# A one-token attention and MLP block on one core: K loads moved between the query-weight loads, wo and w2 loaded in pieces, w2 in longer rows

## The chip, the cores and the metric

The kernel runs on one core of one Trainium2 chip. The metric is the device time of one execution in microseconds (us); lower is better. All runs told here are fast (within 1.5% of the fastest run of the same kernel), and every one of them was compared with runs of the kernel before made in the same rounds on the same chip. A "span" is the time from the first to the last instruction in a profile; it is about 2 us shorter than the measured time of the same run (83.9 against 85.78 before).

## The reference

One new token goes through a pre-norm attention block with a cached window of 4096 keys and values, then through a pre-norm ReLU MLP. Batch and sequence length are 1, the model width D is 512, there are 32 query heads on 8 key/value heads of size 128, and the MLP is 1792 wide. Everything is bf16.

```python
h  = x + attn(layernorm(x))        # q = xn @ wq; softmax(q k^T / sqrt(128)) v; @ wo
h2 = h + relu(layernorm(h) @ w1) @ w2
```

No tensor is used more than once, so the kernel must read all of it: 4.2 MB of wq, 8 x 1.05 MB each of K and V, 4.2 MB of wo, and 1.8 MB each of w1 and w2, together 28.8 MB.

## The kernel before

All loads go out on one queue (SP) in this order, and there are enough buffers (eight shared by wq and K, eight for V) that they are issued well before they are needed (the median K load 19.9 us before it lands):

```python
nc.sync.dma_start(xr_bf[0:1, :], ...)                    # x, 1 KB
for c in range(DC):                                      # wq in four pieces of 1 MB
    nc.sync.dma_start(wq_sb[c], wq_v[:, c, :])
WO_POS = max(Hkv - 2, 0)                                 # 6
for g in range(Hkv):
    if g == WO_POS:
        nc.sync.dma_start(wo_sb[:, :, :], A_wo.rearrange("(c p) n -> p c n", p=P))   # 4 MB, rows of 1 KB
    load_kv(g)                                           # K_g, then V_g, rows of 8 KB
nc.sync.dma_start(w1_sb[:, :, :], B_w1.rearrange("(c p) n -> p c n", p=P))           # rows of 3.5 KB
nc.sync.dma_start(w2_sb[:, :, :], B_w2.rearrange("(c p) n -> p c n", p=P))           # rows of 1 KB
```

(`wq_sb` stands in short for a list of tiles.) The compute, in the order in which it is written; a scheduler at build time decides the order on each engine by when it expects operands to be ready, and the engine then keeps to that order:

```python
... layernorm of x; q: 128 matmuls of wq (weights) by one column, 32 per piece of wq
for g in range(Hkv):
    group_transposes(g)            # T: 32 transposes of K_g on PE, 4 copies on DVE
    if g >= 1: group_pv(g - 1)     # PV: 32 matmuls with V, then the scaling by the inverse sums
    group_scores(g)                # S: 32 matmuls, exp on ACT, sums, inverse, broadcast
    if g == WO_POS:                # hTg: wo matmuls of groups 0 to 5 together (96)
        while wo_done < g: group_wo(wo_done); wo_done += 1
    elif g > WO_POS and wo_done < g:
        group_wo(wo_done); wo_done += 1
group_pv(Hkv - 1)
while wo_done < Hkv: group_wo(wo_done); wo_done += 1
... layernorm of h
... u: 56 matmuls of w1; relu; y: 56 matmuls of w2 into y_ps, reduced; out = y * rstd + h
... transpose to a row; one PSUM tile, first half copied by DVE, second by ACT; store
```

The softmax here doesn't subtract the row's maximum and nothing guards it: scores larger than these inputs give would overflow.

Of the kernel before, what the change touches and what calls it, by code (L numbers as in the profile page):

```python
# [8 lines left out]
BF16 = mybir.dt.bfloat16  # L9
F32 = mybir.dt.float32  # L10
# [6 lines left out]
def kernel(  # L17
# [12 lines left out]
    nc = tc.nc  # L30
    P = nc.NUM_PARTITIONS

    D = A_x.shape[-1]
    Hq, Dh = 32, 128
    _, Hkv, Sk, Dh2 = A_k_cache.shape
# [3 lines left out]
    rep = Hq // Hkv  # L39
    Dff = B_w1.shape[1]  # L40
    DC = D // P
# [3 lines left out]
    NC = W // P  # L45
# [3 lines left out]
    HC = Hq  # L49
    FC = Dff // P  # L50
# [5 lines left out]
    work = ctx.enter_context(tc.tile_pool(name="work", bufs=1))  # L56
    egp = ctx.enter_context(tc.tile_pool(name="egp", bufs=2))
    ktp = ctx.enter_context(tc.tile_pool(name="ktp", bufs=7))
    kx = ctx.enter_context(tc.tile_pool(name="kx", bufs=8))
    vp = ctx.enter_context(tc.tile_pool(name="vp", bufs=8))  # L60
    wp = ctx.enter_context(tc.tile_pool(name="wp", bufs=1))
    psA = ctx.enter_context(tc.tile_pool(name="psA", bufs=1, space=bass.MemoryType.PSUM))
    psT = ctx.enter_context(tc.tile_pool(name="psT", bufs=3, space=bass.MemoryType.PSUM))
    psS = ctx.enter_context(tc.tile_pool(name="psS", bufs=1, space=bass.MemoryType.PSUM))
    psO = ctx.enter_context(tc.tile_pool(name="psO", bufs=3, space=bass.MemoryType.PSUM))
# [2 lines left out]
    nc.sync.dma_start(xr_bf[0:1, :], A_x.flatten_outer_dims()[0:1, :])  # L68

    wq_v = A_wq.rearrange("(c p) n -> p c n", p=P)  # L70
    wq_sb = []
    for c in range(DC):
        t = kx.tile([P, Hq * Dh], BF16, tag="kx")
        nc.sync.dma_start(t[:, :], wq_v[:, c, :])
        wq_sb.append(t)

    wo_sb = wp.tile([P, HC, D], BF16)
    w1_sb = wp.tile([P, DC, Dff], BF16)
    w2_sb = wp.tile([P, FC, D], BF16)

    Ks = [None] * Hkv
    Vs = [None] * Hkv

    def load_kv(g):
        kt = kx.tile([P, NCC, TK * Dh], BF16, tag="kx")
        nc.sync.dma_start(
            kt[:, :, :],
            A_k_cache[0, g, W0:Sk, :].rearrange("(c p t) d -> p c (t d)", p=P, t=TK),
        )
        Ks[g] = kt  # L90
        vt = vp.tile([P, NCC, TK * Dh], BF16, tag="vt")
        nc.sync.dma_start(
            vt[:, :, :],
            A_v_cache[0, g, W0:Sk, :].rearrange("(c p t) d -> p c (t d)", p=P, t=TK),
        )
        Vs[g] = vt

    WO_POS = max(Hkv - 2, 0)
    for g in range(Hkv):
        if g == WO_POS:  # L100
            nc.sync.dma_start(wo_sb[:, :, :], A_wo.rearrange("(c p) n -> p c n", p=P))
        load_kv(g)
    nc.sync.dma_start(w1_sb[:, :, :], B_w1.rearrange("(c p) n -> p c n", p=P))
    nc.sync.dma_start(w2_sb[:, :, :], B_w2.rearrange("(c p) n -> p c n", p=P))

    ident_bf = consts.tile([P, P], BF16)
    make_identity(nc, ident_bf[:])
# [38 lines left out]
    for c in range(DC):  # L146
        nc.tensor.matmul(
            xT_ps[:, c : c + 1], lhsT=xr_bf[0:1, c * P : (c + 1) * P],
            rhs=ones_col_bf[0:1, 0:1], start=True, stop=True,
# [11 lines left out]
    for c in range(DC):  # L161
        for h in range(Hq):
            nc.tensor.matmul(  # L163
                qT_ps[:, c, h : h + 1],
                lhsT=wq_sb[c][:, h * Dh : (h + 1) * Dh],
                rhs=xnT_bf[:, c : c + 1],
                start=True, stop=True,
# [5 lines left out]
    qTs_bf = work.tile([P, Hq], BF16)  # L173
    nc.vector.tensor_scalar(out=qTs_bf[:, :], in0=qT_f[:, :], scalar1=att_scale, scalar2=None, op0=ALU.mult)

    epart = work.tile([P, Hq], F32)
    rtot = work.tile([1, Hq], F32)
    rtot_bf = work.tile([1, Hq], BF16)
# [2 lines left out]
    hT_acc = work.tile([P, DC], F32)  # L181

    E_tiles = [None] * Hkv
    copy_idx = [0]

    kT_blocks_all = [None] * Hkv

    def group_transposes(g):
        kT_blocks = []
        for b in range(NTB):  # L190
            tp = psT.tile([P, TB, P], BF16)
            for i in range(TB):
                ct = b * TB + i
                c, t = divmod(ct, TK)
                nc.tensor.transpose(  # L195
                    tp[:, i, :], Ks[g][:, c, t * Dh : (t + 1) * Dh], ident_bf[:, :],
                )
            ktb = ktp.tile([P, TB, P], BF16)
            nc.vector.tensor_copy(ktb[:, :, :], tp[:, :, :])  # L199
            kT_blocks.append(ktb)  # L200
        kT_blocks_all[g] = kT_blocks

    def group_scores(g):
        kT_blocks = kT_blocks_all[g]
        ST = psS.tile([P, NC, rep], F32)
        for ct in range(NC):
            b, i = divmod(ct, TB)
            nc.tensor.matmul(  # L208
                ST[:, ct, :],
                lhsT=kT_blocks[b][:, i, :],  # L210
                rhs=qTs_bf[:, rep * g : rep * (g + 1)],
                start=True, stop=True,
            )
        E = egp.tile([P, NC, rep], BF16)
        nc.scalar.activation(out=E[:, :, :], in_=ST[:, :, :], func=ACT.Exp)  # L215
        E_tiles[g] = E
        nc.vector.tensor_reduce(  # L217
            out=epart[:, rep * g : rep * (g + 1)],
            in_=E[:, :, :].rearrange("p c j -> p j c"),
            axis=AX.X, op=ALU.add,  # L220
        )
        tot_ps = psA.tile([1, rep], F32, tag="misc")
        nc.tensor.matmul(  # L223
            tot_ps[0:1, :], lhsT=ones_colf[:, 0:1], rhs=epart[:, rep * g : rep * (g + 1)],
            start=True, stop=True,
        )
        nc.vector.reciprocal(rtot[0:1, rep * g : rep * (g + 1)], tot_ps[0:1, :])  # L227
        nc.vector.tensor_copy(rtot_bf[0:1, rep * g : rep * (g + 1)], rtot[0:1, rep * g : rep * (g + 1)])
        bc_ps = psA.tile([P, rep], F32, tag="misc")
        nc.tensor.matmul(  # L230
            bc_ps[:, :], lhsT=ones_row_bf[0:1, :], rhs=rtot_bf[0:1, rep * g : rep * (g + 1)],
            start=True, stop=True,
        )
        nc.vector.tensor_copy(bc_sb[:, rep * g : rep * (g + 1)], bc_ps[:, :])  # L234

    def group_pv(g):
        E = E_tiles[g]
        OT = psO.tile([P, rep], F32, tag="po")
        for ct in range(NC):
            c, t = divmod(ct, TK)  # L240
            nc.tensor.matmul(  # L241
                OT[:, :], lhsT=Vs[g][:, c, t * Dh : (t + 1) * Dh], rhs=E[:, ct, :],
                start=(ct == 0), stop=(ct == NC - 1),
            )
        nc.vector.tensor_tensor(  # L245
            out=OTn_bf[:, rep * g : rep * (g + 1)], in0=OT[:, :],
            in1=bc_sb[:, rep * g : rep * (g + 1)], op=ALU.mult,
        )
    n_hT = [0]

    def group_wo(g):
        hTg = psO.tile([P, DC], F32, tag="po")
        for m in range(DC):
            for j in range(rep):
                h = rep * g + j
                nc.tensor.matmul(  # L256
                    hTg[:, m : m + 1],
                    lhsT=wo_sb[:, h, m * P : (m + 1) * P],
                    rhs=OTn_bf[:, h : h + 1],
                    start=(j == 0), stop=(j == rep - 1),  # L260
                )
        if n_hT[0] == 0:
            nc.vector.tensor_copy(hT_acc[:, :], hTg[:, :])
        else:
            nc.vector.tensor_tensor(out=hT_acc[:, :], in0=hT_acc[:, :], in1=hTg[:, :], op=ALU.add)  # L265
        n_hT[0] += 1

    wo_done = 0
    for g in range(Hkv):
        group_transposes(g)  # L270
        if g >= 1:
            group_pv(g - 1)
        group_scores(g)
        if g == WO_POS:
            while wo_done < g:
                group_wo(wo_done)
                wo_done += 1
        elif g > WO_POS and wo_done < g:
            group_wo(wo_done)
            wo_done += 1  # L280
    group_pv(Hkv - 1)
    while wo_done < Hkv:
        group_wo(wo_done)
        wo_done += 1

    hT_f = work.tile([P, DC], F32)
    nc.vector.tensor_tensor(out=hT_f[:, :], in0=hT_acc[:, :], in1=xT_f[:, :], op=ALU.add)
# [7 lines left out]
    uT_ps = psA.tile([P, DC, FC], F32, tag="misc")  # L295
    for c in range(DC):
        for m in range(FC):
            nc.tensor.matmul(  # L298
                uT_ps[:, c, m : m + 1], lhsT=w1_sb[:, c, m * P : (m + 1) * P],
                rhs=hc_bf[:, c : c + 1], start=True, stop=True,  # L300
            )
    uT_f = work.tile([P, FC], F32)
# [6 lines left out]
    for c in range(FC):  # L309
        for m in range(DC):  # L310
            nc.tensor.matmul(  # L311
                y_ps[:, c, m : m + 1], lhsT=w2_sb[:, c, m * P : (m + 1) * P],
                rhs=uT_bf[:, c : c + 1], start=True, stop=True,
# [5 lines left out]
    outT_bf = work.tile([P, DC], BF16)  # L319
# [1 line left out]
        out=outT_bf[:, :], in0=yT_f[:, :], scalar=rstd2[:, 0:1], in1=hT_f[:, :],  # L321
        op0=ALU.mult, op1=ALU.add,
    )
    orow_ps = psA.tile([1, D], F32, tag="misc")
    for c in range(DC):
        nc.tensor.matmul(  # L326
            orow_ps[0:1, c * P : (c + 1) * P], lhsT=outT_bf[:, c : c + 1], rhs=ident_bf[:, :],
            start=True, stop=True,
        )
    orow_bf = work.tile([1, D], BF16)  # L330
    hD = D // 2
    nc.vector.tensor_copy(orow_bf[0:1, 0:hD], orow_ps[0:1, 0:hD])  # L332
    nc.scalar.copy(orow_bf[0:1, hD:D], orow_ps[0:1, hD:D])  # L333
    nc.sync.dma_start(out.flatten_outer_dims()[0:1, :], orow_bf[0:1, :])


# [28 lines left out]
```

## Time and profile before

| | before |
|---|---|
| time, median of all 15 runs beside the changed kernel | 85.69 us (85.04 to 86.07) |
| span | 83.9 us |
| last byte of K/V, w1, w2 moved | 66.1, 70.6, 75.7 us |
| last landing (completion of w2) | 76.2 us |
| u starts, y ends | 75.9, 79.8 us |

First the slices of the profile page: the span of 83.9 us is cut into 40 slices of 2.1 us, each digit is the busy share in tenths, and the last row is what the DMA engines moved in GB/s.

```profile
PE   0113444079799799799799799869997799637730
DMA  0999999999999999999999999999999999970000
GB/s 0 289 422 422 430 434 422 422 422 418 418 430 418 414 418 426 410 422 414 430 364 348 348 349 354 364 408 422 418 414 413 395 400 363 348 224 6 8 0 0
```

The load stream never rests from 2.1 to about 75 us. It moves at about 420 GB/s, except for one valley of 348 from slice 20 to slice 25 (counted from 0), which is wo with its rows of 1 KB, and a decline at the end, which is w1 and w2. After the stream there are 8 us in which nothing is loaded. PE is lightly used up to slice 7 and nearly full from slice 8 on.

Next the timeline of PE in the kernel before. Columns: start, duration (us), engine, line and operation, output<-inputs, shapes, count, and in brackets how long PE sat idle before it and what ended that.

```profile
13.46 1.01 PE L163 MATMUL qT_ps<-xnT_bf,t 128*128 128x1 bf16 x32 [1.47 <-DMA t<-in_A_wq_dram]
17.38 3.60 PE L195 MATMUL tp<-ident_bf,kt 128*128 128x128 bf16 x32 [2.91 <-DMA kt<-in_A_k_cache_dram]
...
23.89 3.60 PE L195 MATMUL tp<-ident_bf,kt 128*128 128x128 bf16 x32
...
30.40 3.59 PE L195 MATMUL tp<-ident_bf,kt 128*128 128x128 bf16 x32
...
56.71 2.72 PE L256 MATMUL hTg<-OTn_bf,wo_sb 128*128 128x1 bf16 x96 [0.59 <-DMA wo_sb<-in_A_wo_dram]
59.30 3.57 PE L195 MATMUL tp<-ident_bf,kt 128*128 128x128 bf16 x32
...
75.92 1.63 PE L298 MATMUL uT_ps<-hc_bf,w_sb 128*128 128x1 bf16 x56 [0.95 <-DVE hc_bf L291]
78.16 1.63 PE L311 MATMUL y_ps<-uT_bf,w_sb 128*128 128x1 bf16 x56 [0.61 <-DVE uT_bf L307]
```

The transposes of group 0 wait for K0, which stands behind all of wq. From there a group follows every 6.51 us (6.20 once, before group 5), without a wait for data. The one exception: before the transposes of group 6 stand 96 wo matmuls, and they waited 0.59 us for wo. After hT (the last wo matmul ends at 74.1) come the layernorm, u and y, one after the other, all of it behind the end of the stream.

### The profile page before, as it was taken

To read this page: it belongs to the slowest core of one execution; us is meant where nothing else is said; L and a number is where in the kernel's file an instruction comes from. 1 tells how busy PE (TensorE), PEld (TensorE's weight loads), DVE (VectorE), ACT (ScalarE), POOL (GpSimd) and SP (SyncE) were. 2 spreads that over 40 slices of the span, in tenths; PEclk is the share of its full clock that TensorE was granted. 3 is DMA by queue.
4 is the path that set the end of the run, shared out by engine and by line. 5 is a ranking of instruction groups with operands and counts; after the bars stand their busy time and mean duration, and the time that the engine had idled before them with its cause. 6 is when DMAs were issued, how large, how long until landed. Compare 5 with 4: busy or idle time off the path is not lost.

```text
span 83.9 us, 2563 instructions
## 1 busy us (share of the span) xinstructions
PE 58.5 (70%) x1170; PEld 55.1 (66%) x1170; DVE 35.6 (42%) x108; ACT 8.7 (10%) x17; POOL 0.8 (1%) x7
## 2 busy tenths in 40 slices
PE   0113444079799799799799799869997799637730
PEld 0113444079689689689789689759996698527710
DVE  1410000317448538537546646642474366441140
ACT  6160000000100100100100100000001000708010
POOL 4000000000000000000000000000000000000000
PEclk9999999999999999999999985895558957955555
DMA  0999999999999999999999999999999999970000
GB/s 0 289 422 422 430 434 422 422 422 418 418 430 418 414 418 426 410 422 414 430 364 348 348 349 354 364 408 422 418 414 413 395 400 363 348 224 6 8 0 0
DMA packets 9342, 29.00 MB, mean 346 GB/s; under 512 B 370, under 2 KB 6260, under 8 KB 6772
## 3 DMA queue, kind: packets, MB, share of 16 engines
q1 hardware_dynamic: 9332, 28.84, 88.5%
q8 instruction: 9, 0.15, 0.7%
q14 instruction: 1, 0.01, 0.0%
HBM read 28.84 MB, written 0.00 MB: 344 GB/s over the span
## 4 chain that ended last, share of the span: by engine, by line
DMA 66%; PE 21%; DVE 6%; issue 2%; ACT 1%; SPq 0%; DVEq 0%
DMA wo_sb<-in_A_wo_dram 35%; DMA kt<-in_A_k_cache_dram 25%; PE tp L195 8%; DMA t<-in_A_wq_dram 6%; PE hTg L256 5%; PE uT_ps L298 2%; PE y_ps L311 2%; DVE ktb L199 2%; PE OT L241 2%; PE ST L208 1%; PE orow_ps L326 1%; ACT E L215 1%; DVE orow_bf L332 1%; ACT orow_bf L333 0%; DVE rtot L227 0%
## 5 line engine op out<-in xcount | busy, mean ns | idle before, releaser
L195 PE MATMUL tp<-ident_bf,kt 128*128 128x128 bf16 x256 | 28.3, 310 | 2.9 <-DMA kt<-in_A_k_cache_dram 2.9
L195 PEld LDWEIGHTS <-kt 128*128 128x128 bf16 x256 | 26.3, 147 | 3.8 <-DMA kt<-in_A_k_cache_dram 3.0
L199 DVE COPY ktb<-tp 128x1024 bf16<-128x1024 bf16 x32 | 22.0, 692 | 11.0 <-PE tp L195 11.0
L241 PE MATMUL OT<-E,vt 128*128 128x4 bf16 x256 | 9.0, 166 | 2.9 <-ACT E L215 2.9
L241 PEld LDWEIGHTS <-vt 128*128 128x128 bf16 x256 | 8.4, 100 | 3.7 <-issue 3.4
L208 PE MATMUL ST<-qTs_bf,ktb 128*128 128x4 bf16 x256 | 9.4, 167 | 1.5 <-DVE ktb L199 1.5
L208 PEld LDWEIGHTS <-ktb 128*128 128x128 bf16 x256 | 8.8, 104 | 2.2 <-DVE ktb L199 2.2
L163 PE MATMUL qT_ps<-xnT_bf,t 128*128 128x1 bf16 x128 | 4.0, 166 | 7.3 <-DMA t<-in_A_wq_dram 7.3
L215 ACT ACTIVATE E<-ST 128x128 bf16<-128x128 f32 x8 | 2.2, 278 | 63.8 <-PE ST L208 63.8
L163 PEld LDWEIGHTS <-t 128*128 128x128 bf16 x128 | 3.7, 104 | 7.6 <-DMA t<-in_A_wq_dram 7.6
L256 PEld LDWEIGHTS <-wo_sb 128*128 128x128 bf16 x128 | 3.8, 103 | 2.1 <-issue 1.2
L217 DVE TENSOR_REDUCE epart<-E 128x4 f32<-128x128 bf16 x8 | 2.3, 286 | 6.1 <-ACT E L215 6.1
L256 PE MATMUL hTg<-OTn_bf,wo_sb 128*128 128x1 bf16 x128 | 3.8, 165 | 1.5 <-DVE OTn_bf L245 0.9
L170 DVE COPY qT_f<-qT_ps 128x32 f32<-128x32 f32 x1 | 0.2, 192 | 8.6 <-PE qT_ps L163 8.6
L227 DVE RECIPROCAL rtot<-tot_ps 1x4 f32<-1x4 f32 x8 | 1.4, 170 | 4.8 <-PE tot_ps L223 4.8
L298 PEld LDWEIGHTS <-w_sb 128*128 128x128 bf16 x56 | 1.6, 104 | 1.9 <-issue 1.9
L140 ACT ACT_TABLE_LOAD x2 | 2.6, 1283 | 0.7 <-PEq L349 0.7
L142 ACT ACT_TABLE_LOAD x2 | 2.6, 1283 | 0.0
L298 PE MATMUL uT_ps<-hc_bf,w_sb 128*128 128x1 bf16 x56 | 1.6, 165 | 1.0 <-DVE hc_bf L291 1.0
L265 DVE TENSOR_TENSOR hT_acc<-hT_acc,hTg 128x4 f32<-128x4 f32 x7 | 1.1, 159 | 2.6 <-PE hTg L256 2.6
L234 DVE COPY bc_sb<-bc_ps 128x4 f32<-128x4 f32 x8 | 1.3, 162 | 2.0 <-PE bc_ps L230 2.0
L311 PE MATMUL y_ps<-uT_bf,w_sb 128*128 128x1 bf16 x56 | 1.6, 165 | 0.6 <-DVE uT_bf L307 0.6
(46 smaller groups left out, 17.8 us busy)
## 6 DMA issues: line engine op xcount, KB each, us to landing
kt<-in_A_k_cache_dram SPq DMA_DIRECT2D x8, 1024.0 KB, 19.9
vt<-in_A_v_cache_dram SPq DMA_DIRECT2D x8, 1024.0 KB, 18.0
t<-in_A_wq_dram SPq DMA_DIRECT2D x4, 1024.0 KB, 7.9
wo_sb<-in_A_wo_dram SPq DMA_DIRECT2D x1, 4096.0 KB, 29.5
w_sb<-in_B_w_dram SPq DMA_DIRECT2D x2, 1792.0 KB, 20.6
xr_bf<-in_A_x_dram SPq DMA_DIRECT2D x1, 1.0 KB
out_dram<-orow_bf SPq DMA_DIRECT2D x1, 1.0 KB
```

The source lines that it names most:

```text
L140: nc.scalar.activation(out=lv[:, :], in_=negvar[:, :], func=ACT.Ln, bias=eps_t[:, :], scale=-1.0)
L142: nc.scalar.activation(out=rstd[:, :], in_=lv[:, :], func=ACT.Exp, scale=-0.5)
L163: nc.tensor.matmul(qT_ps[:, c, h : h + 1], lhsT=wq_sb[c][:, h * Dh : (h + 1) * Dh], rhs=xnT_bf[:, c : c + 1], start=True, stop=True,)
L195: nc.tensor.transpose(tp[:, i, :], Ks[g][:, c, t * Dh : (t + 1) * Dh], ident_bf[:, :],)
L199: nc.vector.tensor_copy(ktb[:, :, :], tp[:, :, :])
L208: nc.tensor.matmul(ST[:, ct, :], lhsT=kT_blocks[b][:, i, :], rhs=qTs_bf[:, rep * g : rep * (g + 1)], start=True, stop=True,)
L215: nc.scalar.activation(out=E[:, :, :], in_=ST[:, :, :], func=ACT.Exp)
L217: nc.vector.tensor_reduce(out=epart[:, rep * g : rep * (g + 1)], in_=E[:, :, :].rearrange("p c j -> p j c"), axis=AX.X, op=ALU.add,)
L241: nc.tensor.matmul(OT[:, :], lhsT=Vs[g][:, c, t * Dh : (t + 1) * Dh], rhs=E[:, ct, :], start=(ct == 0), stop=(ct == NC - 1),)
L256: nc.tensor.matmul(hTg[:, m : m + 1], lhsT=wo_sb[:, h, m * P : (m + 1) * P], rhs=OTn_bf[:, h : h + 1], start=(j == 0), stop=(j == rep - 1),)
L298: nc.tensor.matmul(uT_ps[:, c, m : m + 1], lhsT=w1_sb[:, c, m * P : (m + 1) * P], rhs=hc_bf[:, c : c + 1], start=True, stop=True,)
L311: nc.tensor.matmul(y_ps[:, c, m : m + 1], lhsT=w2_sb[:, c, m * P : (m + 1) * P], rhs=uT_bf[:, c : c + 1], start=True, stop=True,)
```

## The change

The intent: give PE something to do while wq arrives (K0 and K1 between the pieces of wq), let wo and w2 arrive in pieces near their use, give w2 longer rows, take the sums out of the group's critical order, and let the two output copies run side by side. The core of the diff:

```diff
+        load_k(0); load_wq(0); load_wq(1); load_k(1); load_wq(2); load_wq(3)
+        load_v(0); load_v(1)                               # (cut: the general form)
-        if g == WO_POS:
-            nc.sync.dma_start(wo_sb[:, :, :], ...)
+    wo_after = [4, 5, 6, 7]                                # (cut: computed) one quarter of wo behind V4, V5, V6, V7
     nc.sync.dma_start(w1_sb[:, :, :], B_w1.rearrange("(c p) n -> p c n", p=P))
-    nc.sync.dma_start(w2_sb[:, :, :], B_w2.rearrange("(c p) n -> p c n", p=P))
+    w2_v = B_w2.rearrange("(c p t) n -> p c (t n)", p=P, t=2)
+    for a, b in ((0, 8), (8, 12), (12, FC)):
+        nc.sync.dma_start(
+            w2_sb[:, a:b, :].rearrange("p (c t) n -> p c (t n)", t=2), w2_v[:, a // 2 : b // 2, :]
+        )
...
+    for g in range(Hkv + 2):                               # sums one group later, scaling two groups later
+        if g < Hkv: group_transposes(g)
+        if 1 <= g <= Hkv: group_pv(g - 1)
+        if g < Hkv: group_scores(g)
+        if 1 <= g <= Hkv: group_tot(g - 1)
+        if 2 <= g <= Hkv + 1:
+            group_bcast(g - 2); group_norm(g - 2)
+            ... group_wo(gg) for every normalized gg with g >= wo_after[gg // 2] + 2
...
-                uT_ps[:, c, m : m + 1], lhsT=w1_sb[:, c, m * P : (m + 1) * P],
+                uT_ps[:, c, m : m + 1], lhsT=w1_sb[:, c, (m // 2) * 2 * P + m % 2 : (m // 2 + 1) * 2 * P : 2],
...
-    orow_ps = psA.tile([1, D], F32, tag="misc")
+    orow_a = psA.tile([1, hD], F32, tag="misc")
+    orow_b = psO.tile([1, hD], F32, tag="po")
```

Since a partition now holds rows 2p and 2p+1 of a block of w2, the columns of w1 that make the matching values of u are every second one: the weights of u are read with stride 2. The change also brings a block of warming matmuls in `group_pv`, but with `NDUM = 0` it emits nothing.

More of the change, by code (lines that the diff above doesn't have):

```diff
@@ L70 @@
     wq_v = A_wq.rearrange("(c p) n -> p c n", p=P)
-    wq_sb = []
-    for c in range(DC):
-        t = kx.tile([P, Hq * Dh], BF16, tag="kx")
-        nc.sync.dma_start(t[:, :], wq_v[:, c, :])
-        wq_sb.append(t)
+    wq_sb = [None] * DC
     wo_sb = wp.tile([P, HC, D], BF16)
@@ L82, with load_wq, load_k @@
     Vs = [None] * Hkv
-    def load_kv(g):
+    def load_wq(c):
+        t = kx.tile([P, Hq * Dh], BF16, tag="kx")
+        nc.sync.dma_start(t[:, :], wq_v[:, c, :])
+        wq_sb[c] = t
+    def load_k(g):
         kt = kx.tile([P, NCC, TK * Dh], BF16, tag="kx")
@@ L90, in load_kv, with load_v @@
         Ks[g] = kt
+    def load_v(g):
         vt = vp.tile([P, NCC, TK * Dh], BF16, tag="vt")
@@ L96, in load_kv @@
         Vs[g] = vt
-    WO_POS = max(Hkv - 2, 0)
-    for g in range(Hkv):
-        if g == WO_POS:
-            nc.sync.dma_start(wo_sb[:, :, :], A_wo.rearrange("(c p) n -> p c n", p=P))
-        load_kv(g)
-    nc.sync.dma_start(w1_sb[:, :, :], B_w1.rearrange("(c p) n -> p c n", p=P))
-    nc.sync.dma_start(w2_sb[:, :, :], B_w2.rearrange("(c p) n -> p c n", p=P))
+    NWO = 4 if HC % 4 == 0 else 1
+    HPW = HC // NWO
+    wo_v = A_wo.rearrange("(c p) n -> p c n", p=P)
+    wo_after = [max(0, min(Hkv - 1, Hkv - 1 - (NWO - 1 - i))) for i in range(NWO)]
+    if Hkv >= 2 and DC == 4:
+        load_k(0); load_wq(0); load_wq(1); load_k(1); load_wq(2); load_wq(3)
+        load_v(0)
+        for i in range(NWO):
+            if wo_after[i] == 0:
+                nc.sync.dma_start(wo_sb[:, i * HPW : (i + 1) * HPW, :], wo_v[:, i * HPW : (i + 1) * HPW, :])
+        load_v(1)
+        for i in range(NWO):
+            if wo_after[i] == 1:
+                nc.sync.dma_start(wo_sb[:, i * HPW : (i + 1) * HPW, :], wo_v[:, i * HPW : (i + 1) * HPW, :])
+        start_g = 2
+    else:
+        for c in range(DC):
+            load_wq(c)
+        start_g = 0
+    for g in range(start_g, Hkv):
+        load_k(g)
+        load_v(g)
+        for i in range(NWO):
+            if wo_after[i] == g:
+                nc.sync.dma_start(wo_sb[:, i * HPW : (i + 1) * HPW, :], wo_v[:, i * HPW : (i + 1) * HPW, :])
+    nc.sync.dma_start(w1_sb[:, :, :], B_w1.rearrange("(c p) n -> p c n", p=P))
+    w2_v = B_w2.rearrange("(c p t) n -> p c (t n)", p=P, t=2)
[3 more added lines that the diff above has]
+        )
     ident_bf = consts.tile([P, P], BF16)
@@ L174 @@
     nc.vector.tensor_scalar(out=qTs_bf[:, :], in0=qT_f[:, :], scalar1=att_scale, scalar2=None, op0=ALU.mult)
+    warm_sink = work.tile([P, 1], F32)
     epart = work.tile([P, Hq], F32)
@@ L183 @@
     E_tiles = [None] * Hkv
+    OT_tiles = [None] * Hkv
     copy_idx = [0]
@@ L204, in group_scores @@
         kT_blocks = kT_blocks_all[g]
-        ST = psS.tile([P, NC, rep], F32)
+        ST = psS.tile([P, NC, rep], F32, tag="ST")
         for ct in range(NC):
@@ L221, in group_scores, with group_tot @@
         )
+    def group_tot(g):
         tot_ps = psA.tile([1, rep], F32, tag="misc")
@@ L228, in group_scores, with group_bcast @@
         nc.vector.tensor_copy(rtot_bf[0:1, rep * g : rep * (g + 1)], rtot[0:1, rep * g : rep * (g + 1)])
+    def group_bcast(g):
         bc_ps = psA.tile([P, rep], F32, tag="misc")
@@ L234, in group_scores @@
         nc.vector.tensor_copy(bc_sb[:, rep * g : rep * (g + 1)], bc_ps[:, :])
+    NDUM = 0
     def group_pv(g):
         E = E_tiles[g]
+        if NDUM > 0:
+            wps = psS.tile([P, 512], F32, tag="ST")
+            for i in range(NDUM):
+                nc.tensor.matmul(
+                    wps[:, :], lhsT=ident_bf[:, :], rhs=Vs[g][:, 0, 0:512],
+                    start=(i == 0), stop=(i == NDUM - 1),
+                )
+            nc.vector.tensor_copy(warm_sink[:, :], wps[:, 0:1])
         OT = psO.tile([P, rep], F32, tag="po")
@@ L244, in group_pv, with group_norm @@
             )
+        OT_tiles[g] = OT
+    def group_norm(g):
+        OT = OT_tiles[g]
         nc.vector.tensor_tensor(
@@ L266, in group_wo, with try_wo @@
         n_hT[0] += 1
-    wo_done = 0
-    for g in range(Hkv):
-        group_transposes(g)
-        if g >= 1:
-            group_pv(g - 1)
-        group_scores(g)
-        if g == WO_POS:
-            while wo_done < g:
-                group_wo(wo_done)
-                wo_done += 1
-        elif g > WO_POS and wo_done < g:
-            group_wo(wo_done)
-            wo_done += 1
-    group_pv(Hkv - 1)
-    while wo_done < Hkv:
-        group_wo(wo_done)
-        wo_done += 1
+    stage = {g: 0 for g in range(Hkv)}
+    normalized = []
+    wo_emitted = set()
+    def try_wo(wo_available: bool):
+        if not wo_available:
+            return
+        for gg in list(normalized):
+            if gg not in wo_emitted:
+                group_wo(gg)
+                wo_emitted.add(gg)
+                normalized.remove(gg)
+    for g in range(Hkv + 2):
+        if g < Hkv:
+            group_transposes(g)
+        if 1 <= g <= Hkv:
+            group_pv(g - 1)
+        if g < Hkv:
+            group_scores(g)
+        if 1 <= g <= Hkv:
+            group_tot(g - 1)
+        if 2 <= g <= Hkv + 1:
+            group_bcast(g - 2)
+            group_norm(g - 2)
+            normalized.append(g - 2)
+            for gg in list(normalized):
+                if g >= wo_after[(rep * gg) // HPW] + 2:
+                    group_wo(gg)
+                    normalized.remove(gg)
+    try_wo(True)
     hT_f = work.tile([P, DC], F32)
@@ L323 @@
     )
-    orow_ps = psA.tile([1, D], F32, tag="misc")
+    hD = D // 2
+    orow_bf = work.tile([1, D], BF16)
+    orow_a = psA.tile([1, hD], F32, tag="misc")
+    orow_b = psO.tile([1, hD], F32, tag="po")
     for c in range(DC):
+        half, k = (orow_a, c) if c < DC // 2 else (orow_b, c - DC // 2)
         nc.tensor.matmul(
-            orow_ps[0:1, c * P : (c + 1) * P], lhsT=outT_bf[:, c : c + 1], rhs=ident_bf[:, :],
+            half[0:1, k * P : (k + 1) * P], lhsT=outT_bf[:, c : c + 1], rhs=ident_bf[:, :],
             start=True, stop=True,
         )
-    orow_bf = work.tile([1, D], BF16)
-    hD = D // 2
-    nc.vector.tensor_copy(orow_bf[0:1, 0:hD], orow_ps[0:1, 0:hD])
-    nc.scalar.copy(orow_bf[0:1, hD:D], orow_ps[0:1, hD:D])
+    nc.scalar.copy(orow_bf[0:1, 0:hD], orow_a[0:1, :])
+    nc.vector.tensor_copy(orow_bf[0:1, hD:D], orow_b[0:1, :])
     nc.sync.dma_start(out.flatten_outer_dims()[0:1, :], orow_bf[0:1, :])
```

## The prediction

> **What bounds the kernel now.** Two chains end together. The DMA table (busy tenths, GB/s by slice) shows the 16 queues nine tenths busy from 2.1 us on; the transfer records give the last K/V packet at 66.1, the last of w1 at 70.6, of w2 at 75.7 us. Rows of 8 KB (311 ns a packet) move at about 420 GB/s, the 3.5 KB rows of w1 (142 ns) at 400, the 1 KB rows of wo and w2 (49 ns) at 347: wo takes 42.3 to 56.1.
> In the timeline of PE, q waits for each 1 MB piece of wq (2.49 us apart, 1.0 of work); transposes start at 17.4, when K0 lands; then PE is in step: 6.51 us a group (transposes 3.4, scores 1.4, 0.36 waiting for exp, PV and small matmuls 1.3), eight groups plus 4.5 of wo work, to 74.1. Then come, serially, LN2 (1.8), u (75.9 to 77.6), y (78.2 to 79.8), the row, two copies in turn (0.42 + 0.36) and the output: 8.2 us of tail after the last weight byte.
>
> **What the change does.**
> 1. K0 and K1 go between the wq pieces. By the present spacing K0 lands near 6, K1 near 13.4, wq3 near 18.4. T0 and three quarters of T1 (seven ktp buffers), 6 us, fill holes where PE now waits for wq. PE's work left from 19.4, at today's durations and stalls: 3.1 + 4 + 6 x 6.5 + 4.0 = 50 us, so hT at about 69.5 instead of 74.3.
> 2. wo in four pieces, same 1 KB rows: no faster.
> 3. w2 in 2 KB rows: a line through 142 and 311 ns gives 86 ns a packet (estimate), 4.8 instead of 5.4 us. The stream gains only that: it ends near 75.1, semaphore near 75.6.
> 4. The tail moves under the stream: LN2 ends near 71.2, u near 73; w2 chunks are multiplied as they land. After the last piece 8 of 56 y matmuls remain (0.35 us).
> 5. The halves of the row get own PSUM tiles and copy side by side: -0.36.
> 6. w1's weights are read with stride 2. The Trainium skill, "TensorE: Matmul & The Clock Gate", Weight-path perf modes, gives the fast weight load's read pattern as packed or strided; so u should keep its 29.5 ns a matmul. No run here shows it yet.
>
> **On the critical path.** The stream becomes the only bound. End = 75.6 + 0.35 + (83.87 - 79.81 - 0.36 = 3.7) = 79.7 us of span, against 83.9: 4.2 less. The 5 us that PE gains are what lets the tail move (slack about 2 us), not a second gain. Time: 85.86 - 4.2 = 81.7 us, range 80.6 to 83.8. Chances: faster by over 2% 0.91, within 2% 0.07, slower by over 2% 0.02.
>
> **What would show it.** Timeline of PE: transposes of g0 near 6 us, before the q matmuls; hT near 69 to 70; u done before the last w2 byte; the last y matmuls waiting for DMA. Chain of waits: ends with DMA w2, y, row, output. DMA table: 420 with four valleys of 347, stream end near 75.
>
> **What would make it wrong.** The compiled PE order follows simulated readiness; with T0 behind q, PE starts at 19.4 and nothing is gained (about 85). Strided weight loads at half rate: u +1.7 us. PE lagging over 2 us at the last group. Issue waits that idle the queues. 2 KB rows no faster: +0.6.

## The result, and the profile after

The changed kernel takes 81.69 us (median of 12 runs, 81.48 to 82.05), the kernel before 85.69 us (15 runs). The ratio is 0.9538, 95% interval 0.9515 to 0.9561. Ratios in this document are the mean time of one kernel's fast runs over the mean time of the fast runs of the kernel before of the same rounds, so they are not quite the ratio of the medians quoted beside them.

The same three rows of the page, after; a slice is now 2.0 us.

```profile
PE   0205796973488897899699698879887978735830
DMA  0899999999999999999999999999999999999300
GB/s 1 258 406 439 414 443 410 443 406 435 410 431 423 418 414 435 402 414 396 357 411 403 409 349 407 406 405 355 397 418 410 354 376 403 398 388 354 120 0 1
```

PE now works from slice 2 on. The one wide valley has become four narrow ones (357, 349, 355, 354), one for each quarter of wo. The stream ends at almost the same time as before, 75.1 us, but after it there are only 4.7 us left instead of 8.2.

The timeline of PE after, with the lines that answer to those shown of before:

```profile
5.99 1.14 PE L225 MATMUL tp<-ident_bf,kt 128*128 128x128 bf16 x9 [2.92 <-DMA kt<-in_A_k_cache_dram]
8.46 1.01 PE L190 MATMUL qT_ps<-xnT_bf,t 128*128 128x1 bf16 x32 [1.34 <-DMA t<-in_A_wq_dram]
9.34 2.61 PE L225 MATMUL tp<-ident_bf,kt 128*128 128x128 bf16 x23
11.74 1.04 PE L190 MATMUL qT_ps<-xnT_bf,t 128*128 128x1 bf16 x32
13.43 3.36 PE L225 MATMUL tp<-ident_bf,kt 128*128 128x128 bf16 x32 [0.64 <-DMA kt<-in_A_k_cache_dram]
...
52.96 3.60 PE L225 MATMUL tp<-ident_bf,kt 128*128 128x128 bf16 x32 [0.42 <-DMA kt<-in_A_k_cache_dram]
...
60.99 3.46 PE L225 MATMUL tp<-ident_bf,kt 128*128 128x128 bf16 x32 [0.59 <-DMA kt<-in_A_k_cache_dram]
...
71.30 1.63 PE L359 MATMUL uT_ps<-hc_bf,w_sb 128*128 128x1 bf16 x56 [0.95 <-DVE hc_bf L352]
73.77 1.01 PE L372 MATMUL y_ps<-uT_bf,w_sb 128*128 128x1 bf16 x32 [0.84 <-DMA w_sb<-in_B_w_dram]
75.05 1.01 PE L372 MATMUL y_ps<-uT_bf,w_sb 128*128 128x1 bf16 x24 [0.26 <-DMA w_sb<-in_B_w_dram]
```

The transposes of groups 0 and 1 are done before wq is complete. In groups 6 and 7 the transposes wait for K6 and K7, so in this run PE has caught up with the stream. y waits twice for w2: for the first piece, and for the second.

The end of the chain of waits, after (start, duration, what):

```profile
61.63 13.38 DMA w_sb<-in_B_w_dram
75.00 0.04 issue
75.05 0.59 PE y_ps L372 x16
75.64 0.04 issue
75.68 0.39 PE y_ps L372 x8
76.07 0.02 issue
76.09 0.23 DVE yT_f L377
```

The chain hangs on the loads of w2 up to 75.0; the last 8 of the 56 y matmuls start at 75.68, just after the last piece. The last landing in the transfer records is 75.64. In the kernel before, the same chain went through the wo matmuls, the last two groups, the layernorm, u and y.

When the loads are complete, by the completion records of the two traces (us):

```
          K0    wq0    K1    K6     K7     w1     w2, by pieces
before  17.33   5.95  22.15  59.15  64.10  71.13  76.18
after    5.94   8.42  13.38  52.92  60.95  71.05  73.73  75.00  75.64
```

The number came out as predicted, and that it did so this closely is partly luck: the span became 4.0 us shorter and not 4.2, and the prediction started from a run of 85.86 us, 0.17 above the median. Nor does the number show that it came for the reasons given: the change has six parts, and a tie of several chains can hide which of them matters. The experiments take the change apart.

### The profile page after: what moved, and what is told of

It reads as the page before. It is cut to its first block, busy times and chain, and to the rows that moved or that the text cites. A ratio compares the mean times of both kernels' runs of the same rounds, so it can differ in the third digit from the quotient of the medians.

```text
span 79.9 us, 2566 instructions
## 1 busy us (share of the span) xinstructions
PE 56.7 (71%) x1170; PEld 53.1 (66%) x1170; DVE 34.7 (43%) x108; ACT 8.7 (11%) x17; POOL 0.8 (1%) x7
## 4 chain that ended last, share of the span: by engine, by line
DMA 49%; PE 25%; SPq 13%; DVE 6%; issue 2%; ACT 1%; DVEq 0%
DMA kt<-in_A_k_cache_dram 32%; DMA w_sb<-in_B_w_dram 17%; PE tp L225 15%; SPq L126 7%; PE OT L284 5%; DVE ktb L229 4%; SPq L129 4%; PE ST L238 2%; SPq L94 2%; ACT E L245 1%; PE y_ps L372 1%; DVE rtot L258 1%; PE bc_ps L263 1%; SPq L125 1%; DVE orow_bf L396 1%
## 5 line engine op out<-in xcount | busy, mean ns | idle before, releaser
L225 PE MATMUL tp<-ident_bf,kt 128*128 128x128 bf16 x256 | 26.9, 298 | 5.0 <-DMA kt<-in_A_k_cache_dram 5.0
L225 PEld LDWEIGHTS <-kt 128*128 128x128 bf16 x256 | 24.8, 140 | 6.4 <-DMA kt<-in_A_k_cache_dram 5.4
L238 PE MATMUL ST<-qTs_bf,ktb 128*128 128x4 bf16 x256 | 8.9, 166 | 2.6 <-DVE qTs_bf L201 1.2
L238 PEld LDWEIGHTS <-ktb 128*128 128x128 bf16 x256 | 8.3, 102 | 3.3 <-issue 1.6
L284 PEld LDWEIGHTS <-vt 128*128 128x128 bf16 x256 | 7.6, 99 | 2.9 <-issue 2.9
L284 PE MATMUL OT<-E,vt 128*128 128x4 bf16 x256 | 7.7, 165 | 2.2 <-ACT E L245 2.2
L303 PE MATMUL hTg<-OTn_bf,wo_sb 128*128 128x1 bf16 x128 | 4.5, 165 | 0.4
L359 PEld LDWEIGHTS <-w_sb 128*128 128x128 bf16 x56 | 1.6, 104 | 1.9 <-DMA w_sb<-in_B_w_dram 1.9
L372 PEld LDWEIGHTS <-w_sb 128*128 128x128 bf16 x56 | 1.7, 105 | 1.4 <-DMA w_sb<-in_B_w_dram 1.3
L263 PE MATMUL bc_ps<-rtot_bf,ones_row_bf 1*128 1x4 bf16 x8 | 1.4, 169 | 1.0 <-DVE rtot L258 1.0
## 6 DMA issues: line engine op xcount, KB each, us to landing
w_sb<-in_B_w_dram SPq DMA_DIRECT2D x1, 512.0 KB, 13.4
```

The lines of the kernel that those rows point to most:

```text
L225: nc.tensor.transpose(tp[:, i, :], Ks[g][:, c, t * Dh : (t + 1) * Dh], ident_bf[:, :],)
L238: nc.tensor.matmul(ST[:, ct, :], lhsT=kT_blocks[b][:, i, :], rhs=qTs_bf[:, rep * g : rep * (g + 1)], start=True, stop=True,)
L284: nc.tensor.matmul(OT[:, :], lhsT=Vs[g][:, c, t * Dh : (t + 1) * Dh], rhs=E[:, ct, :], start=(ct == 0), stop=(ct == NC - 1),)
L303: nc.tensor.matmul(hTg[:, m : m + 1], lhsT=wo_sb[:, h, m * P : (m + 1) * P], rhs=OTn_bf[:, h : h + 1], start=(j == 0), stop=(j == rep - 1),)
L359: nc.tensor.matmul(uT_ps[:, c, m : m + 1], lhsT=w1_sb[:, c, (m // 2) * 2 * P + m % 2 : (m // 2 + 1) * 2 * P : 2], rhs=hc_bf[:, c : c + 1], ...
L372: nc.tensor.matmul(y_ps[:, c, m : m + 1], lhsT=w2_sb[:, c, m * P : (m + 1) * P], rhs=uT_bf[:, c : c + 1], start=True, stop=True,)
```

## The experiments

The theory tested: the load stream is the bound after the change; PE's early start only makes room for the tail (layernorm, u, most of y) to run under the stream. Rivals: that the early start of PE is itself the gain; or that the pieces, rows and copies are, and the early start is idle.

All runs gave results that were accepted as correct. The table is in the order told; "lost" in the text is against the median of the changed kernel, 81.69 us, which was run in other rounds: differences below half a microsecond (e4, e5) are not separated by the intervals of the ratios alone, and rest on the traces beside them. e5, e8 and e10 also ran on another chip than the other experiments. The edits are shown shortened, in places with words for several lines.

| run | what | median us | ratio to before, 95% interval |
|---|---|---|---|
| e1 | before + early K only | 85.74 | 0.9983 (0.9942 to 1.0025) |
| e12 | before + early K + wo in pieces | 83.87 | 0.9780 (0.9756 to 0.9804) |
| e2 | after without early K | 83.52 | 0.9734 (0.9680 to 0.9787) |
| e6 | after with wo in one load | 87.14 | 1.0138 (1.0093 to 1.0182) |
| e7 | after with half of the transposes | 81.84 | 0.9530 (0.9499 to 0.9561) |
| e3 | after with w2 in one load | 83.11 | 0.9682 (0.9655 to 0.9708) |
| e4 | after with w2 rows of 1 KB | 82.06 | 0.9562 (0.9540 to 0.9585) |
| e5 | after with one row tile | 81.99 | 0.9563 (0.9545 to 0.9581) |
| e9 | after with 14 rows of w2 per partition | 82.91 | 0.9681 (0.9641 to 0.9720) |
| e8 | after with x from ACT's queue | 81.35 | 0.9487 (0.9470 to 0.9505) |
| e10 | attempt at a faster version | 81.07 | 0.9453 (0.9435 to 0.9471) |
| e13 | e10 with wo matmuls released earlier | 81.21 | 0.9481 (0.9439 to 0.9524) |

### e1: only the early K loads

```diff
 # on the kernel before
-    wq0 wq1 wq2 wq3   K0 V0 K1 V1   K2 V2 ... K5 V5  wo  K6 V6 K7 V7
+    K0 wq0 wq1 K1 wq2 wq3   V0 V1   K2 V2 ... K5 V5  wo  K6 V6 K7 V7
```

> The kernel before with only the early K0 and K1 loads; wo stays one 4 MB load before K6, w2 one load, old group order. Theory A (the early start of PE is turned into time only because wo comes in pieces): PE starts near 6 us instead of 17.4, but the 96 hTg matmuls stand before the transposes of group 6 in PE's order and wait for wo, which still lands near 56.7; from there everything runs as in the kernel before, hT near 74.3, time the same as before within 0.3 us (85.5 to 86.0). Rival B (the PE head start is the gain by itself): hT near 70, and with w2 landing at 76.2 the y matmuls end near 77.9 instead of 79.8, time 83.6 to 83.9.

Measured: 85.74 us, no change. In its profile PE starts the transposes at 5.96 us as in the changed kernel and keeps its lead up to the end of group 5, and then gives all of it back in one wait. Timeline of PE of e1:

```profile
51.56 0.16 PE L236 MATMUL bc_ps<-rtot_bf,ones_row_bf 1*128 1x4 bf16 x1
56.63 2.72 PE L262 MATMUL hTg<-OTn_bf,wo_sb 128*128 128x1 bf16 x96 [4.91 <-DMA wo_sb<-in_A_wo_dram]
59.21 3.36 PE L201 MATMUL tp<-ident_bf,kt 128*128 128x128 bf16 x32
```

Compare the second line with its twin in the kernel before: there the wait was 0.59 us, here it is 4.91, and the matmuls start at the same time (56.71 and 56.63). Theory A held to the letter: the engine's order is fixed, and the next thing in it needed 4 MB of wo. An early start alone was worth nothing.

### e12: early K and wo in pieces

```diff
 # on e1
-            nc.sync.dma_start(wo_sb[:, :, :], ...)          # before K6
+        if g >= 4: load quarter g - 4 of wo                 # behind V4, V5, V6, V7
-        if g == WO_POS: all wo matmuls so far
+        while wo_done < g and g >= 4 + wo_done // 2 + 2: group_wo(wo_done); wo_done += 1
```

> The kernel of e1 (early K0 and K1) with wo in four pieces behind V4 to V7 and its matmuls spread over the groups; w2 one load of 1 KB rows, sums not deferred, one row tile, as in the kernel before. Theory: PE's lead now survives, hT near 70, but y waits for the single w2 load, which lands at 76.1 as in the kernel before; y ends near 77.8 instead of 79.8, time 83.5 to 84.0: about half of the gain. Rival (deferring the sums carries part of the PE gain): hT at 71.5 or later.

Measured: 83.87 us. Timeline of PE of e12:

```profile
71.42 1.64 PE L301 MATMUL uT_ps<-hc_bf,w_sb 128*128 128x1 bf16 x56 [0.94 <-DMA w_sb<-in_B_w_dram]
76.34 1.66 PE L314 MATMUL y_ps<-uT_bf,w_sb 128*128 128x1 bf16 x56 [3.29 <-DMA w_sb<-in_B_w_dram]
```

u starts at 71.42, as early as in the changed kernel (71.30), although the sums are not deferred here: deferring them carried nothing that this shows. (The wait is put down to w1, which landed at 71.31; u's other operand was ready at 71.27, so PE's own chain would have led to the same start.) Then y waits 3.29 us for the single load of w2. So PE's part of the change moves PE's own chain by 4.5 us, and the stream takes back more than half of it.

### e2: everything except the early K loads

```diff
 # on the changed kernel
-        load_k(0); load_wq(0); load_wq(1); load_k(1); load_wq(2); load_wq(3)
-        load_v(0)
+        load_wq(0); load_wq(1); load_wq(2); load_wq(3)
+        load_k(0); load_v(0); load_k(1)
```

> The changed kernel with wq0 to wq3 loaded first again. Theory: the stream ends at 75.1 as in the changed kernel and w2 lands by 75.7, but PE starts at 17.4 and is the bound: T7 near 65, hT near 73.5, u ends near 76.7, y runs without waiting for w2 and ends near 78.8, time 84.2 to 84.8 (2.5 to 3 us over the changed kernel, about 1.3 under the one before). Rival (the gain is in the load pieces and rows and the copies): within 0.5 us of 81.7.

Measured: 83.52 us, so 1.8 us lost, less than the 2.5 to 3 expected. The profile shows the expected kind of run, PE late and w2 waiting for it. Timeline of PE of e2:

```profile
75.92 1.63 PE L372 MATMUL y_ps<-uT_bf,w_sb 128*128 128x1 bf16 x56 [0.61 <-DVE uT_bf L368]
```

w2 was complete at 75.75, before y began; y waited only for DVE and ran in one piece. The size was off because PE got through its groups in about 6.2 us instead of the 6.5 of the kernel before. Already the first group, with transposes of the same 3.59 us, took 6.17 instead of 6.51, since the next transposes did not come behind a broadcast there; from then on a broadcast stands before them again, and what was gained came from faster transposes (3.26 us in group 1, 2.88 in group 4, instead of 3.6). The profile is of the fastest of the four runs (83.16, 83.20, 83.84, 83.96), so it says nothing of why the slower two came nearer to the expected 84.2.

### e6: wo in one load again

```diff
 # on the changed kernel
-    NWO = 4
-    wo_after = [4, 5, 6, 7]
+    NWO = 1
+    wo_after = [5]            # one load of 4 MB before K6, as in the kernel before
```

> The changed kernel with wo as one load before K6, as in the kernel before. Theory: the stream as a whole is no longer (end 75.1), but K6 lands near 59.2 and K7 near 64.1 instead of 52.9 and 61.0, and the hTg work of all groups falls after wo, so hT is near 75 to 76 and the time 85.5 to 87, the whole gain gone. Rival (wo in pieces only changes when wo arrives, PE has slack for it): within 1 us of 81.7.

Measured: 87.14 us, 1.4% slower than the kernel before. Timeline of PE of e6:

```profile
59.27 3.60 PE L225 MATMUL tp<-ident_bf,kt 128*128 128x128 bf16 x32 [7.34 <-DMA kt<-in_A_k_cache_dram]
```

PE waits 7.34 us for K6, which lands at 59.23 behind 4 MB of wo instead of at 52.92, and the wo matmuls pile up behind it (u starts at 77.76). Not all of the 5.5 us lost is the place of wo in the stream. wo had landed at 56.75, but in this kernel its matmuls stand behind the scores of group 6 or later, where e1 runs 96 of them before group 6. The transposes of group 6 start at nearly the same time in both (59.27 and 59.21), and u 2.3 us later here than in e1 (77.76 and 75.48): about that much goes with the order of the matmuls, which no run tested alone. In both runs the gain is gone. No byte less is moved when wo comes in quarters; what is gained is that K6 and K7 no longer stand behind all of it.

### e7: half of the transposes

```diff
 # on the changed kernel; a wrong result on purpose
         for b in range(NTB):
+            if b % 2 == 1:
+                kT_blocks.append(kT_blocks[-1])
+                continue
```

> The changed kernel with every second block of transposes and its copy left out (wrong result on purpose: scores of odd blocks use the block before). PE does 128 transposes less, about 13 us of its work. Theory (the load stream is the only bound): last w2 piece lands at 75.6 as before, the last 8 y matmuls wait for it, time 81.4 to 81.8, at most 0.3 us under the changed kernel. Rival (PE is still a bound or tied with it): 2 us or more faster.

Measured: 81.84 us, no faster. PE was busy for 46.6 us instead of 56.7 and DVE for 23.9 instead of 34.7, and the time stayed. Timeline of PE of e7:

```profile
61.22 1.89 PE L228 MATMUL tp<-ident_bf,kt 128*128 128x128 bf16 x16 [1.97 <-DMA kt<-in_A_k_cache_dram]
...
71.22 1.65 PE L362 MATMUL uT_ps<-hc_bf,w_sb 128*128 128x1 bf16 x56 [1.90 <-DMA w_sb<-in_B_w_dram]
73.92 1.01 PE L375 MATMUL y_ps<-uT_bf,w_sb 128*128 128x1 bf16 x32 [1.05 <-DMA w_sb<-in_B_w_dram]
75.16 1.03 PE L375 MATMUL y_ps<-uT_bf,w_sb 128*128 128x1 bf16 x24 [0.23 <-DMA w_sb<-in_B_w_dram]
```

Every stage at the end now waits for its load, and starts within 0.25 us of when it did in the changed kernel (61.22 against 60.99, 71.22 against 71.30, 73.92 against 73.77, 75.16 against 75.05). This is the plainest evidence for the stream: 10 us of PE's work taken away changed nothing. (The result passed the comparison although half of the scores were of the wrong keys; that comparison is not sensitive to them.)

### e3: w2 in one load

```diff
 # on the changed kernel
-    for a, b in ((0, 8), (8, 12), (12, FC)):
+    for a, b in ((0, FC),):
```

> The changed kernel with w2 as one load of 2 KB rows. Theory: it lands near 75.7, y's 56 matmuls (1.65 us) start then and end near 77.4 instead of 76.1, so 1.3 us slower than the changed kernel: 82.7 to 83.2. Rival (the pieces matter little): within 0.4 us of 81.7.

Measured: 83.11 us, so 1.4 us lost. w2 landed at 75.69, and all 56 y matmuls ran from 75.74. The pieces are worth what they hide, most of y.

### e4: w2 in rows of 1 KB, w1 read contiguously

```diff
 # on the changed kernel
-    w2_v = B_w2.rearrange("(c p t) n -> p c (t n)", p=P, t=2)
+    w2_v = B_w2.rearrange("(c p) n -> p c n", p=P)
-    lhsT=w1_sb[:, c, (m // 2) * 2 * P + m % 2 : (m // 2 + 1) * 2 * P : 2]
+    lhsT=w1_sb[:, c, m * P : (m + 1) * P]
```

> The changed kernel with w2 in the same three pieces but 1 KB rows, and w1's weights read contiguously. Theory: stream ends at 75.7 instead of 75.15, time 0.4 to 0.6 us over the changed kernel (82.1 to 82.3); u takes the same 1.63 us with contiguous weights as with stride 2. Rival (the row size does nothing): equal within 0.1 us, packets summing to the same time.

Measured: 82.06 us, 0.37 lost; the last packet moved at 75.57 instead of 75.14 us, and the last piece landed at 76.07 instead of 75.64. u took 1.63 us with either layout.

### e5: the row in one tile again

```diff
 # on the changed kernel
-    orow_a = psA.tile([1, hD], ...); orow_b = psO.tile([1, hD], ...)
+    orow_ps = psA.tile([1, D], ...)
-    nc.scalar.copy(first half); nc.vector.tensor_copy(second half)
+    nc.vector.tensor_copy(first half); nc.scalar.copy(second half)
```

> The changed kernel with the output row in one PSUM tile again and its two copies as before. Theory: the copies run in turn (0.42 + 0.36), so 0.36 to 0.4 us slower than the changed kernel, 82.05 to 82.1. Rival (the copies were not in series for the tile's sake): no difference.

Measured: 81.99 us, 0.30 lost. The ACT copy again waited for the DVE copy (it began at 77.73, 0.04 after DVE's end). In the traces the last copy ends at 78.09 instead of 77.73, so 0.36 later, as predicted; the 0.30 of the medians, from other rounds and another chip, is no finer than that.

### e9: more of w2 in one run, weights at a longer stride

```diff
 # on the changed kernel
-    w2_v = B_w2.rearrange("(c p t) n -> p c (t n)", p=P, t=2)
+    w2_v = B_w2.rearrange("(p t) n -> p (t n)", t=FC)         # runs of 8, 4 and 2 KB for the three pieces
-    lhsT=w1_sb[:, c, (m // 2) * 2 * P + m % 2 : (m // 2 + 1) * 2 * P : 2]
+    lhsT=w1_sb[:, c, m : Dff : FC]                            # stride 14
```

> The changed kernel with 14 consecutive rows of w2 on a partition, so the three pieces move in runs of 8, 4 and 2 KB, and w1's weights are read with stride 14 (28 bytes). Theory: 8 rows a queue at 311 + 161 + 86 ns give 4.46 us instead of 4.76, stream end 0.3 us earlier, time 81.3 to 81.5 if u keeps its 1.63 us. Rival (a stride of 28 bytes slows the weight load): u takes 3 us or more and the time is 81.7 or higher.

Measured: 82.91 us, 1.2 slower than the changed kernel. The load did what the theory said: the last piece landed at 75.41 instead of 75.64. But the rival was right about u. Timeline of PE of e9:

```profile
71.50 3.49 PE L359 MATMUL uT_ps<-hc_bf,w_sb 128*128 128x1 bf16 x56 [0.95 <-DVE hc_bf L352]
75.60 1.63 PE L372 MATMUL y_ps<-uT_bf,w_sb 128*128 128x1 bf16 x56 [0.61 <-DVE uT_bf L368]
```

u took 3.49 us instead of 1.63: the starts of its matmuls are 60 ns apart with stride 14, and 27 ns apart with stride 1 or 2. A gain of 0.23 us in the stream cost 1.86 on PE, more than PE's slack.

### e8: x from another queue

```diff
 # on the changed kernel
-    nc.sync.dma_start(xr_bf[0:1, :], ...)
+    nc.scalar.dma_start(xr_bf[0:1, :], ...)
```

> The changed kernel with one line changed: the 1 KB load of x is issued from the ACT queue, so the stream of the SP queue starts about 0.35 us earlier. Theory (every landing up to the last sets the end): all landings and the time 0.3 to 0.4 us earlier, 81.3 to 81.4. Rival (the start is not the stream's limit, or x arriving beside K0 delays the rest): 81.7 as before.

Measured: 81.35 us (81.32 to 81.37), 0.34 faster, as expected. The first packet of K0 moved at 1.75 instead of 2.10 us, K7 landed at 60.63 instead of 60.95 and the last piece of w2 at 75.26 instead of 75.64. A kilobyte that stood first in the queue delayed the whole stream by about the time of its issue (0.32 us on SP). Timeline of PE of e8:

```profile
74.09 1.63 PE L372 MATMUL y_ps<-uT_bf,w_sb 128*128 128x1 bf16 x56 [0.61 <-DVE uT_bf L368]
```

Here y no longer waits for w2: it runs in one piece behind u, and its last 8 matmuls start at 75.37, 0.1 us after the last landing. In this profile PE and the stream are already tied. The Trainium skill, "DMA: Bandwidth & Descriptors", Issuing engines are not separate DMA queues, says that issuing from several engines saves only the sequencer's time to initiate a load, usually small beside the load itself. This run agrees, and shows when that small time counts: at the head of a stream that is never idle afterwards.

### e10: an attempt at a faster version

```diff
 # on e8
-    for a, b in ((0, 8), (8, 12), (12, FC)):  rows of 2 KB
+    for a, b, t in ((0, 8, 4), (8, 12, 4), (12, FC, 2)):  runs of t rows, 4 KB, 4 KB and 2 KB
-    lhsT=w1_sb[..., stride 2]
+    lhsT=w1_sb[..., stride 4 for m < 12, else 2]
-    y_ps over all 14 chunks; yT_f = sum; outT = yT_f * rstd + h
+    y_ps over 12 chunks; yT_f = sum; yh = yT_f * rstd + h
+    y2_ps over the last 2 chunks (accumulated); outT = y2_ps * rstd + yh
```

> An attempt at a faster version: the changed kernel with x from the ACT queue, w2 in runs of 4 KB for its first twelve chunks (w1's weights then read with stride 4, 8 bytes), and y's first twelve chunks summed, scaled and added to h while the last two chunks land, so one DVE step is left after them. Theory: 0.35 + 0.24 + 0.25, so 80.8 to 81.1, u at 1.63 us if a stride of 8 bytes is still free. Rival (8 bytes already slow the weight load): u at 2.5 us or more, and 81.3 or higher.

Measured: 81.07 us. Five of the six runs lie between 80.98 and 81.08, and the sixth, which is the profiled one, took 81.98. Against the kernel before, the interval (0.9435 to 0.9471) lies below that of the changed kernel (0.9515 to 0.9561), so it is faster than that, by 0.6 us in the medians; the two were not in the same rounds. From e13 (below) it is not separated. Timeline of PE of its profiled run, the slowest of the six:

```profile
61.56 3.57 PE L225 MATMUL tp<-ident_bf,kt 128*128 128x128 bf16 x32
...
71.95 1.95 PE L360 MATMUL uT_ps<-hc_bf,w_sb 128*128 128x1 bf16 x56 [0.95 <-DVE hc_bf L352]
74.51 1.55 PE L374 MATMUL y_ps<-uT_bf,w_sb 128*128 128x1 bf16 x48 [0.61 <-DVE uT_bf L369]
```

Two things stand out. u took 1.95 us: 33 ns between starts for stride 4, so neither the theory's 27 nor as slow as the rival's. And group 7 began at 61.56 without waiting, though K7 had landed at 60.81 (as in e8: 61.32 and 60.63); w2's last piece landed at 75.18 while y was still running. In this run PE was the bound.

### e13: the wo matmuls earlier

```diff
 # on e10
-                if g >= wo_after[(rep * gg) // HPW] + 2:
+                if g >= wo_after[(rep * gg) // HPW] + 1:
```

> The combined version of e10 (x from the ACT queue, w2 in runs of 4 KB, y summed in two parts), with the wo matmuls of each pair of groups released one group earlier, so that only 32 instead of 64 of them stand behind the last PV. What it tells apart: in e10's profile PE was late by 0.3 us or more when the last w2 piece landed, so PE and the stream were nearly tied there. Theory: with 1 us of PE work taken out of the end, u ends before the first w2 piece lands, y waits for the last piece in every run, and the full 0.35 + 0.24 + 0.25 is gained: 80.7 to 80.9, narrow spread. Rival (the stream is the only bound already): same as e10, 81.0 to 81.1.

Measured: 81.21 us (81.02 to 81.83, two of six runs at 81.8). No gain; the theory behind this run failed. In its profile group 7 starts at 62.14 and PE has no wait for data after the start of group 2. Moving 32 matmuls from behind the last PV to a place before group 5 only moved the work, since PE was full there too. What the run does show is that the time of e10 and e13 is no longer set by the stream alone. What decides between the fast and the slow runs of the same kernel stays open: both profiles that were taken are of the slower runs of their kernel. In e10's every group from 1 on took 3.57 to 3.60 us for its transposes, and in e13's all but two did, of which the fast one (2.01 us, group 1) stands where PE then waits for wq. The profile of the changed kernel has one group of 2.59 and one of 3.22, which would be enough; but no profile of a fast run was taken to set beside them. The mean granted clock is a hint and no proof: e10's slow run reads 0.93 and its fast ones 0.71 to 0.73, but e13's two slow runs read 0.66 and 0.91.

## Why the prediction was right, point by point

- **What bounded the kernel before (two chains that end together).** Right as far as it went, but it missed the third party. The stream and PE both ended near 75, and e1 shows that wo itself was a third bound at 56.7: the wait of 0.59 us was the tip of one of 4.91.
- **Step 1, the early K loads.** K0 landed at 5.94 (predicted near 6), K1 at 13.38 (13.4), wq3 at 19.59 (18.4), hT was summed by 69.9 (69.5). All of T1 fitted into the gap, not three quarters: its 32 transposes into PSUM ended at 16.8, and only the copy of the last quarter to SBUF waited, until 22.18.
- **Step 2, "wo in four pieces, same 1 KB rows: no faster".** True of the stream, and misleading as a valuation. e6 loses 5.5 us without this part (some 2.3 of them with the order of its matmuls), and e1 gains nothing without it. The sum for PE in step 1 (no wait for wo) silently took it for granted.
- **Step 3, the rows of 2 KB.** 85 ns a packet against 86 estimated; stream end 75.14 against 75.1; last landing 75.64 against 75.6; worth 0.37 us in e4 against 0.6.
- **Step 4, the tail under the stream.** The layernorm ended at 71.2 and u at 72.9, as said, and the last 8 y matmuls began right behind the last landing. e3 shows 1.4 us for the pieces of w2, e2 shows 1.8 us for having u done in time.
- **Step 5, the copies.** 0.36 us in the traces of e5 and the changed kernel, as predicted; 0.30 in the medians.
- **Step 6, the stride.** u kept its 27 ns from start to start (the 29.5 of the prediction is the stage's length over its count). The Trainium skill, "TensorE: Matmul & The Clock Gate", Weight-path perf modes, lists the read pattern as packed or strided; stride 2 kept the pace here, but e9 shows that not every stride does.
- **"The stream becomes the only bound ... slack about 2 us".** The first half held in e7. The slack was mis-sized: in the profiled run y could have started by 74.4 without delaying the end (75.64 + 0.39 - 1.63) and u's result was ready at 73.4, so it was 1.0 us. There PE reached group 7 in time to wait for K7. In the profiles of e4 and e8, which give PE the same work, it reached that group 0.7 us after K7 had landed, and the same sum gives 0.4 us (74.83 against 74.44) and 0.1 (74.02 against 73.94). So PE is a second bound, in these profiles 1.0 us or less behind the stream. e9 overdrew the slack by a long way, and in e10 and e13 a gain of half a microsecond in the stream was enough to make PE the bound in some runs.

The prediction's total, 4.2 us, was nearly met (4.0 in the medians), and the experiments confirm the mechanism it named: PE's gain (u starts 4.6 us earlier, 71.30 against 75.92) is not additive with the stream's, it only buys the overlap. The parts don't sum: early K alone gives 0, the rest without it 2.3 (e2), and together they give 4.0.

## What to carry to other kernels

An engine that runs a fixed order turns a head start into time only if every later wait in that order moves too: before moving a load forward, list the next large load that the engine needs, and see whether a short wait there is short only because the engine used to come late. When two chains tie, price each change by both, and expect the parts of a change to be worth nothing alone; a test that removes half of one engine's work tells in one run whether that engine is still a bound. Under a load stream that never rests, what is left to win is at its ends: what is issued first, and how little work remains behind the last piece.

## What the Trainium skill lacked or had wrong

- "TensorE: Matmul & The Clock Gate", Weight-path perf modes, gives the fast weight load as packed or strided and names no cost of a stride. Measured here with one-column matmuls: 27 ns from start to start at strides of 1 and 2 bf16 elements (the changed kernel and e4), 33 at stride 4 (e10), 60 at stride 14 (e9).
- "SBUF — State Buffer", Door 1, says of its 16-byte lines that bf16 can be strided by up to 8 elements for free, with a hint that two hits a line are needed. For weight loads stride 4 already cost 22% (27 to 33 ns). Strides of 3 and of 5 to 13 were not run.
- "DMA: Bandwidth & Descriptors", Specifications, gives about 358 GB/s as the limit of HBM for one core, and the page's Bandwidth section says that it binds for loads from HBM, although the same section notes that this is the share with both cores of a pair streaming and measured 425 for one alone. This stream, on one core, moved at about 420 GB/s for some 40 us with rows of 8 KB. The Specifications also call transfers of 512 B and more enough for line rate; here a packet took 311 ns for 8 KB, 145 for 3.5 KB, 85 for 2 KB and 48 to 49 for 1 KB, which is about 420, 395, 385 and 335 to 340 GB/s over 16 engines.
- "TensorE: Matmul & The Clock Gate", Part 1, warns that clock events in a trace are unreliable and gives 107 ns as the cold and 56 ns as the warm pace of 128-column matmuls. It does not say what their absence looks like. In e7 and e8 the mean granted clock reads 1.0, no change of it having been recorded, and yet 32 transposes of e8 took 3.57 us; in the changed kernel 32 transposes took 3.36 us at 13.4 where the clock reads 1.0 and 3.60 us at 53.0 where it reads 0.5. Judge by the pace: in the changed kernel 202 of 247 intervals between the starts of neighbouring transposes were 106 to 107 ns, the page's cold pace, and 31 were 55 to 56.
